# Seven products of halves in batch 1 as well, with the state read and the next scores moved behind stage 1's second tile

## The chip, the cores and the metric

The kernel runs on one core of one Trainium2 chip. The metric is the device time of one execution in microseconds. TensorE multiplies matrices, VectorE and ScalarE do elementwise work and empty TensorE's result banks, SyncE (SP) and ScalarE issue DMAs, and the 16 DMA engines move the data.

## The reference

For each of 8 batches there is an attention of 512 tokens and 32 states in 8 heads of 64, both ways, and then a bilinear layer over all rows (tokens and states, 4608 of them):

```
scores  = x @ state.T / 8          # softmax over the states
xread   = softmax(scores) @ state
scores2 = state @ x.T / 8          # softmax over the tokens
sread   = softmax(scores2) @ x
rows    = concat(xread, sread)     # (4608, 512)
out     = ((rows @ w1) * (rows @ w2)) @ w3 @ w_out
```

The weights come as float64; the result is float32.

## The kernel before

**Products.** A float32 operand is split into two parts of a 32-bit format that TensorE takes at a higher rate: `split` makes `hi` by a cast on ScalarE (L97) and `lo` by a subtraction on VectorE (L98). One product of two operands is then three matmuls (lo by hi, hi by hi, hi by lo).

**Before the batches.** The weights are loaded and turned into float32 in a pool `pro` that is closed later, w3 @ w_out is multiplied once (`w34`, L542 and L555) and kept split as `wo`.

**A batch.** The attention of a batch (`attention_steps`) is a generator in steps: the scores as matmuls (`per_head`, L147), then softmax steps on VectorE and ScalarE (L187 to L216), then `at_hi` and `at_lo` (L221, L97, L98), and last a transpose of the other softmax (L228), whose blocks sixteen DMAs on SP put in their places (`move_blocks`, L171). The read of the state (`read_state`, L243) multiplies these blocks by the batch's tokens `x_s`; its result goes through two VectorE operations and sixteen more DMAs on SP into `sread`. The token softmax never meets the state alone: `sw_steps` multiplies state by w1 and w2 (four units, L147), and stage 1 multiplies `at` by that.

Stage 1 (`stage1_sums`, L310) makes 8 feature tiles of 128 features by 512 tokens, 12 matmuls each for w1 and w2 together; ScalarE copies one half out of the bank, and VectorE multiplies it by the other. Three pairs of banks (`two_banks`) go round among stage 1, the scores and the `sw_steps` units. Stage 2 multiplies the features by `wo`.

Batches 0 and 1 do stage 2 plainly: four token tiles of 24 matmuls of 512 columns (`stage2`, L324). Batches 2 to 7 (`fast_batch`) do it in seven products of halves (`stage2_quarters`, `product`, L428), Winograd's form of Strassen's scheme, with 24 matmuls of 256 columns each. That needs sums and differences of the features' quarters (S1 to S4, on VectorE) and of the weights' quarters (`combine_weights`, four calls in all, L371 and L377).

**Order.** TensorE and SP execute in the order in which the program traces their instructions. VectorE and ScalarE are ordered by a planner that goes by program order, readiness and priority; `high_priority` lifts the emptying of a bank.

In batch 0's stage 2 the side work of batch 1 stands between the token tiles (`side_steps(1)`): scores earlier, then batch 0's read, units 0 and 1, then the rest of batch 1's softmax with its block moves, then units 2 and 3. After the last token tile come the loads of batch 1's tokens (`load_tokens(1)`, L159) and of batch 2's `st` and `x_d` (`load_x(2)`, L153, L155). In batch 1 the read, the scores of batch 2 and all units stand behind stage 2's first token tile. In batches 2 to 7 the read, the next scores and the next loads stand behind stage 1's fourth tile, softmax steps behind the fifth and seventh, units 0 and 1 behind stage 2's first product, followed by the last softmax step, and units 2 and 3 behind the second product.

After batch 7, `state_rows` passes all 256 state rows through the same layer (L661, L662, L324).

Of the kernel before, what the change touches and what calls it, by code (L numbers as in the profile page):

```python
# [35 lines left out]
WARM = 15  # L36
PLAIN = 2

@with_exitstack
def attn_bilinear_kernel(  # L40
# [53 lines left out]
    def split(hi, lo, src):  # L94

        return (
            nc.scalar.copy(out=hi, in_=src),  # L97
            nc.vector.tensor_tensor(out=lo, in0=src, in1=hi.bitcast(F32), op=ALU.subtract),  # L98
        )
# [242 lines left out]

    def side_steps(b):


        if b == B:
            return [[reads[b - 1]], [], [], []]
        scores, reads[b], a2 = attention_steps(b)
        w = sw_steps(b)
        softmax = scores()  # L350
        first = partial(islice, softmax, 3)
        if b == 1:
            def rest():

                with tc.issue_after(stored[0].ins):
                    yield from softmax

            return [[first], [reads[0], w[0], w[1]], [], [rest], [w[2], w[3]], []]

        product = partial(islice, softmax, 1)  # L360
        loads = [partial(load_tokens, b), partial(load_x, b + 1)]
        return [[w[0], w[1], product, reads[b - 1], *loads, w[2], w[3], lambda: softmax], [], [], []]

# [3 lines left out]
    def combine_weights(k):  # L367

        raw = [tmp_tile() for _ in range(2)]
        for i, whole in enumerate(raw):  # L370
            nc.vector.tensor_tensor(  # L371
                out=whole, in0=wo["hi"][:, i * QF + k].bitcast(F32), in1=wo["lo"][:, i * QF + k].bitcast(F32), op=ALU.add
            )
        b11, b12, b21, b22 = (whole[:, half * HO:(half + 1) * HO] for whole in raw for half in range(2))
        t = late.tile([P, QF, HO], F32, name="r22")
        for j, (x, y) in enumerate(((b12, b11), (b22, t[:, 0]), (b22, b12), (b21, t[:, 1]))):
            nc.vector.tensor_tensor(out=t[:, j], in0=x, in1=y, op=ALU.subtract)  # L377
# [10 lines left out]

    def hidden_quarters(ps, ft, q):
        a_sb = tmp_tile()  # L390
        p, kk = divmod(ft, 2)
        first, second = slice(0, HT), slice(HT, S)
        with tc.high_priority():
            nc.scalar.copy(out=a_sb, in_=ps[:, 0])  # L394
            if ft < QF:
                if kk == 0:
                    q["raw"].append(main.tile([P, 2, NF], F32, name="g_x", bufs=2))
                nc.vector.tensor_tensor(out=q["raw"][p][:, kk], in0=a_sb, in1=ps[:, 1], op=ALU.mult)  # L398
            else:
                if ft == QF:  # L400
                    q["r22"] = late.tile([P, QF, HT], F32, name="r22")
                nc.vector.tensor_tensor(out=a_sb[:, first], in0=a_sb[:, first], in1=ps[:, 1, first], op=ALU.mult)  # L402
                nc.vector.tensor_tensor(out=q["r22"][:, ft - QF], in0=a_sb[:, second], in1=ps[:, 1, second], op=ALU.mult)
# [4 lines left out]
        if ft >= QF:  # L408
            split(*(t[:, kk] for t in q["a12"][p - 2]), a_sb[:, first])
            if kk:  # L410
                i = p - 2
                raw, r22 = q["raw"][i], q["r22"][:, 2 * i:2 * i + 2]
                nc.vector.tensor_tensor(out=raw[:, :, second], in0=raw[:, :, second], in1=r22, op=ALU.add)
                nc.vector.tensor_tensor(out=raw[:, :, first], in0=raw[:, :, second], in1=raw[:, :, first], op=ALU.subtract)
        elif kk:
            raw = q["raw"][p]
# [3 lines left out]
            split(*q["s3"][p], s3)  # L420

    def product(ps, a, w, fresh):
# [10 lines left out]

    def stage2_quarters(b, q, units):
        half = lambda o: slice(o * HO, (o + 1) * HO)
# [5 lines left out]
        def stored_quarter(o, rows, cols):  # L441
            for tt in range(2):
                first = (2 * rows + tt) * P
                nc.scalar.dma_start(out=out[b, first:first + P, half(cols)], in_=o[:, half(tt)])
# [9 lines left out]
        for i in range(2):  # L454
            split(*a22[i], q["r22"][:, 2 * i:2 * i + 2])
# [5 lines left out]
        s = [raw[:, :, 0:HT] for raw in q["raw"]]  # L461
        for i in range(2):
            split(*s2[i], s[i])
        product(bank_e, a22, t_part(3), False)
        for i in range(2):
            hi, lo = (t.bitcast(F32) for t in q["a12"][i])
            nc.vector.tensor_tensor(out=s[i], in0=hi, in1=s[i], op=ALU.subtract)  # L467
            nc.vector.tensor_tensor(out=s[i], in0=lo, in1=s[i], op=ALU.add)
        s1 = quarter_pairs()
        for i in range(2):  # L470
            split(*s1[i], q["raw"][i][:, :, HT:S])
        bank_d = two_banks()[:, 0]
# [5 lines left out]
        for i in range(2):  # L478
            last_split[:] = split(*s4[i], s[i])
        bank_c = bank()  # L480
# [8 lines left out]

    def fast_batch(b):  # L490
        q = {"raw": []}
        softmax = iter(())
        for ft in range(FT):
            hidden_quarters(stage1_sums(b, ft), ft, q)
# [20 lines left out]
    def batch_stage2(b, gs):  # L515
        side = side_steps(b + 1)
        for tt in range(NT):
            stage2(gs, tt, [(out[b, tt * P:(tt + 1) * P], 0, P)])
            run(side[tt])
            if tt in (1, 2):  # L520
                combine_weights(tt + 1)


    with tc.tile_pool(name="pro", bufs=2) as pro:
# [90 lines left out]
        for quarter in range(QT):  # L615
# [5 lines left out]
            if quarter == 1:  # L621
                side = side_steps(1)
            elif quarter == 2:
                run(side.pop(0))
# [7 lines left out]
        early_stage2(QT - 1)  # L632
        for tt in range(NT):
            dests = [(out[0, tt * P:(tt + 1) * P], 0, P)]
            if tt in early:
                store(acc[tt], dests)
            else:
                stage2(gs, tt, dests)
            run(side[tt])
        load_tokens(1)  # L640
        load_x(2)
    late = ctx.enter_context(tc.tile_pool(name="late", bufs=1))
    t_parts = {part: late.tile([P, 4, QF, HO], F32R, name=f"t_{part}") for part in ("hi", "lo")}


    def state_rows():
# [5 lines left out]
        for ft in range(FT):  # L652
            quarter, c = divmod(ft * P, NQ)
            ps = two_banks()
            for i in range(2):
# [7 lines left out]
            gs.append([g[:, :n] for g in new_g(ft)])  # L663
# [4 lines left out]
            nc.vector.tensor_tensor(out=sums[:, 0], in0=sums[:, 0], in1=sums[:, 1], op=ALU.mult)  # L668
            split(*gs[-1], sums[:, 0])
# [4 lines left out]
    for b in range(1, PLAIN):  # L674
        gs = []
        for ft in range(FT):
            stage1(b, ft, gs)
            if ft % 4 == 3:
                combine_weights(ft // 4)
        batch_stage2(b, gs)  # L680
    for b in range(PLAIN, B):
        fast_batch(b)
    with tc.issue_after(last_split[0].ins), tc.issue_after(last_split[1].ins):
# [45 lines left out]
```

## Time and profile before

| | |
|---|---|
| median of three runs | 497.1 us (496.81 to 497.45) |
| the profiled execution, its own time | 496.68 us |
| its span, first to last instruction | 494.9 us |
| mean granted TensorE clock | 0.999 |
| TensorE busy | 486.4 us (98%) |
| VectorE busy | 375.3 us (76%) |
| ScalarE busy | 238.8 us (48%) |

All times in the views are microseconds from the span's start, and about 1.8 us of the execution lie outside the span. "PE" is TensorE's matmuls, "PEld" its weight loads, "DVE" VectorE, "ACT" ScalarE, "SPq" the DMAs that SP issues. In the chain of waits, each row is a piece of the chain that ended last, with its start and its length. A timeline row has start, length, engine, line, operation, the tile written and those read, shapes and a count; in brackets stands how long the engine was idle before and what ended that. A row of groups ends with busy time, the mean ns of one, and the idle time before.

### The profile page before, as it was taken

The numbers are of one execution on the slowest core, as the hardware profiler recorded it, in microseconds if no ns is written. First come the engines' busy times: TensorE is split into PE (matmuls) and PEld (weight loads), VectorE is DVE, ScalarE is ACT, GpSimd is POOL, SyncE is SP. The second block draws the span as 40 slices with busy tenths as digits, with TensorE's granted clock in tenths as the row PEclk, the third lists the DMA queues.
The fourth block names the chain that finished last, engine by engine and source line by source line (L and its number), as shares of the span: only waits on it lengthen the run. The fifth ranks groups of instructions, "written<-read, shape, count | busy, mean of one in ns | idle before, by whom it ended". The sixth has DMA issues, their size and how long they took to land.

```text
span 494.9 us, 8790 instructions
## 1 busy us (share of the span) xinstructions
PE 486.4 (98%) x3486; PEld 376.0 (76%) x3486; DVE 375.3 (76%) x584; ACT 238.8 (48%) x371; POOL 0.2 (0%) x4
## 2 busy tenths in 40 slices
PE   8999999999999999999999999999999999999996
PEld 5444467777876868897789778977897888899885
DVE  5669896772679889956995799479948994687770
ACT  4767784443544346613651365137513751453650
POOL 0000000000000000000000000000000000000000
PEclk9999999999999999999999999999999999999999
DMA  8996971013500721430233033303330222001101
GB/s 340 363 386 228 366 280 31 13 47 77 187 8 19 235 50 41 160 110 3 88 114 108 2 110 99 101 3 107 112 90 2 91 52 78 4 3 46 42 1 42
DMA packets 55785, 52.48 MB, mean 106 GB/s; under 512 B 42688, under 2 KB 49856, under 8 KB 51136
## 3 DMA queue, kind: packets, MB, share of 16 engines
q1 hardware_dynamic: 47488, 43.27, 26.6%
q10 hardware_dynamic: 8256, 8.65, 5.0%
q8 instruction: 27, 0.44, 0.4%
q14 instruction: 14, 0.11, 0.1%
HBM read 38.27 MB, written 8.91 MB: 95 GB/s over the span
## 4 chain that ended last, share of the span: by engine, by line
PE 83%; DVE 9%; DMA 3%; ACT 2%; issue 1%; SPq 1%; ACTq 0%; DVEq 0%
PE ps L310 29%; PE ps_o L428 20%; PE ps_o L324 8%; PE ps L147 6%; PE ps_o L555 6%; PE ps L661 3%; PE ps L428 3%; PE ps_o L542 3%; PE ps L542 3%; DMA e<-work 2%; PE ps L662 2%; DVE work L187 1%; DVE m L204 1%; DVE m L190 1%; SPq L171 1%
## 5 line engine op out<-in xcount | busy, mean ns | idle before, releaser
L310 PE MATMUL ps<-at_lo,sw_hi 128*128 128x512 f32 x256 | 101.2, 395 | 0.8 <-ACT g_hi L97 0.8
L310 PE MATMUL ps<-at_hi,sw_hi 128*128 128x512 f32 x256 | 99.7, 390 | 0.0
L310 PE MATMUL ps<-at_hi,sw_lo 128*128 128x512 f32 x256 | 99.6, 389 | 0.0
L394 ACT COPY tmp<-ps 128x512 f32<-128x512 f32 x48 | 28.1, 588 | 89.1 <-PE ps L310 54.4
L310 PEld LDWEIGHTS ps<-at_lo,sw_hi 128*128 128x128 f32 x256 | 48.1, 188 | 17.3 <-DVE g_x L398 3.4
L310 PEld LDWEIGHTS ps<-at_hi,sw_lo 128*128 128x128 f32 x256 | 48.1, 188 | 10.1
L310 PEld LDWEIGHTS ps<-at_hi,sw_hi 128*128 128x128 f32 x256 | 48.1, 188 | 9.6 <-issue 0.2
L97 ACT CAST g_hi<-g_x 128x512 fp32r<-128x512 f32 x48 | 29.2, 621 | 39.5 <-DVE g_x L467 20.4
L398 DVE TENSOR_TENSOR g_x<-tmp,ps 128x512 f32<-128x512 f32 x24 | 16.4, 687 | 36.2 <-ACT tmp L394 36.2
L97 ACT CAST g_hi<-tmp 128x256 fp32r<-128x256 f32 (+1 forms) x54 | 27.1, 503 | 32.4 <-DVE tmp L402 16.8
L98 DVE TENSOR_TENSOR sw_lo<-ps,sw_hi 128x1024 fp32r<-128x1024 f32 (+1 forms) x34 | 38.3, 1149 | 5.2 <-ACT sw_hi L97 5.2
L98 DVE TENSOR_TENSOR g_lo<-g_x,g_hi 128x512 fp32r<-128x512 f32 x48 | 31.6, 682 | 3.1 <-ACT g_hi L97 2.8
L98 DVE TENSOR_TENSOR g_lo<-tmp,g_hi 128x256 fp32r<-128x256 f32 (+1 forms) x54 | 28.8, 535 | 6.2 <-ACT g_hi L97 5.6
L97 ACT CAST sw_hi<-ps 128x1024 fp32r<-128x1024 f32 (+1 forms) x34 | 31.3, 967 | 4.2 <-PE ps L147 4.1
L147 PE MATMUL ps<-w_sb,st 64*32 64x512 f32 (+1 forms) x544 | 31.4, 570 | 0.0
L428 PE MATMUL ps_o<-wo_lo,g_hi 128*128 128x256 f32 x144 | 29.6, 287 | 0.5 <-DVE tmp L438 0.5
L428 PE MATMUL ps_o<-t_lo,g_hi 128*128 128x256 f32 x144 | 29.5, 287 | 0.0
L428 PE MATMUL ps_o<-t_hi,g_hi 128*128 128x256 f32 x144 | 29.0, 283 | 0.0
L428 PE MATMUL ps_o<-wo_hi,g_hi 128*128 128x256 f32 x144 | 29.0, 283 | 0.0
L428 PE MATMUL ps_o<-wo_hi,g_lo 128*128 128x256 f32 x144 | 29.0, 283 | 0.0
L428 PE MATMUL ps_o<-t_hi,g_lo 128*128 128x256 f32 x144 | 29.0, 283 | 0.0
L555 PE MATMUL ps_o<-w_sb,w 128*128 128x512 f32 x64 | 28.5, 599 | 0.0
(113 smaller groups left out, 912.6 us busy)
## 6 DMA issues: line engine op xcount, KB each, us to landing
raw<-in_w_k_dram SPq DMA_DIRECT2D x8, 1024.0 KB, 6.8
x_d<-in_x_d_dram SPq DMA_DIRECT2D x8, 1024.0 KB, 7.0
raw<-in_w_dram SPq DMA_DIRECT2D x8, 1024.0 KB, 6.4
x_s<-in_x_s_dram SPq DMA_DIRECT2D x8, 1024.0 KB, 5.3
out_dram<-tmp ACTq DMA_DIRECT2D x48, 128.0 KB, 2.0
raw<-in_w3t_dram SPq DMA_DIRECT2D x4, 1024.0 KB, 7.5
e<-work SPq DMA_DIRECT2D x96, 32.0 KB, 2.0
sread<-turned SPq DMA_DIRECT2D x128, 4.0 KB, 1.7
```

The costliest lines, as they stand in the source:

```text
L97: nc.scalar.copy(out=hi, in_=src),
L98: nc.vector.tensor_tensor(out=lo, in0=src, in1=hi.bitcast(F32), op=ALU.subtract),
L147: nc.tensor.matmul(ps[j * NS:(j + 1) * NS, q], sts[b][rows, j], moving(rows, j), start=True, stop=True)
L310: nc.tensor.matmul(ps[:, i], w[:, kt, c:c + P], a[:, kt], start=(k == 0), stop=(k == 3 * KT - 1))
L324: nc.tensor.matmul(ps[:, :DO], g, wo[w][:, ft, :], start=(ft == 0 and k == 0), stop=(ft == FT - 1 and k == 2))
L394: nc.scalar.copy(out=a_sb, in_=ps[:, 0])
L398: nc.vector.tensor_tensor(out=q["raw"][p][:, kk], in0=a_sb, in1=ps[:, 1], op=ALU.mult)
L428: nc.tensor.matmul(ps[:, tt * HO:(tt + 1) * HO], g[:, tt * P:(tt + 1) * P], w(part, k), start=(fresh and k == 0 and n == 0 and tt == 0), s ...
L542: nc.tensor.matmul(w34_ps[i][:, :DO], chunks[k][:, DO + i * P:DO + (i + 1) * P], w_out[k], start=(k == 0), stop=(k == FT - 1),)
L555: nc.tensor.matmul(w34_ps[i][:, :DO], w3s[i][:, k * P:(k + 1) * P], w_out[k], start=(k == 0), stop=(k == FT - 1))
L661: nc.tensor.matmul(ps[:, i], wh[:, ks], sr[:, kt], start=(kt == 0), stop=False)
L662: nc.tensor.matmul(ps[:, i, :n], wl[:, ks], sr[:, kt, 1], start=False, stop=(kt == NP - 1))
```

## The change

`PLAIN` goes from 2 to 1, so batch 1 takes the seven products, and the path for plain batches after batch 0 goes away. The function for the others is now `quarter_batch`:

- The read of the batch and the scores and loads of the next stand behind stage 1's second tile, and softmax steps behind the third and the fifth.
- The last softmax step, with the block moves, stands behind units 2 and 3.
- Feature tiles 4 to 7 are multiplied whole into a tile of their own, `late`'s `raw`, and their first halves are split two at a time. S4 is one subtraction per pair in stage 1, in place of two in stage 2 (L467, L468).
- The pool `late` opens ahead of batch 0's stage 2, where three of the four weight combinations now stand, one behind each of its first three token tiles. The fourth stands behind the second tile of batch 1.
- The loads `load_tokens(1)` and `load_x(2)` still follow batch 0's stage 2. The loads in later batches move with the read.

```
-PLAIN = 2
+PLAIN = 1
...
-        t = late.tile([P, QF, HO], F32, name="r22")
+        t = late.tile([P, QF, S], F32, name="raw")[:, :, :HO]
...
-    def hidden_quarters(ps, ft, q):
-        a_sb = tmp_tile()
+    def hidden_quarters(a, b, ft, q):
...
+        if ft == QF:
+            q["late"] = late.tile([P, QF, S], F32, name="raw")
+        elif ft < QF and kk == 0:
+            q["raw"].append(main.tile([P, 2, NF], F32, name="g_x", bufs=2))
+        whole = q["raw"][p][:, kk] if ft < QF else q["late"][:, ft - QF]
         with tc.high_priority():
...
-                nc.vector.tensor_tensor(out=a_sb[:, first], in0=a_sb[:, first], in1=ps[:, 1, first], op=ALU.mult)
-                nc.vector.tensor_tensor(out=q["r22"][:, ft - QF], in0=a_sb[:, second], in1=ps[:, 1, second], op=ALU.mult)
+            nc.vector.tensor_tensor(out=whole, in0=a, in1=b, op=ALU.mult)
...
+            split(*q["a12"][i], half[:, :, first])
+            nc.vector.tensor_tensor(out=raw[:, :, second], in0=raw[:, :, second], in1=half[:, :, second], op=ALU.add)
+            nc.vector.tensor_tensor(out=raw[:, :, first], in0=raw[:, :, second], in1=raw[:, :, first], op=ALU.subtract)
+            nc.vector.tensor_tensor(out=half[:, :, first], in0=half[:, :, first], in1=raw[:, :, first], op=ALU.subtract)
...
-        run(units[:3])
+        run(units)
...
-        run(units[3:])
+        run(more)
...
-        for i in range(2):
-            hi, lo = (t.bitcast(F32) for t in q["a12"][i])
-            nc.vector.tensor_tensor(out=s[i], in0=hi, in1=s[i], op=ALU.subtract)
-            nc.vector.tensor_tensor(out=s[i], in0=lo, in1=s[i], op=ALU.add)
...
-    def fast_batch(b):
+    def quarter_batch(b):
         q = {"raw": []}
+        w = sw_steps(b + 1) if b + 1 < B else [lambda: None] * 4
...
-            if ft == QF - 1:
+            if ft == 1:
                 reads[b]()
                 if b + 1 < B:
                     scores, reads[b + 1], _ = attention_steps(b + 1)
...
-            elif ft in (QF, QF + 2):
+            elif ft in (2, 4):
                 next(softmax, None)
-
-        units = sw_steps(b + 1) if b + 1 < B else []
-        stage2_quarters(b, q, units[:2] + [lambda: softmax] + units[2:])
+            if b == PLAIN and ft == 1:
+                combine_weights(QF - 1)
+        stage2_quarters(b, q, w[:2], [*w[2:], lambda: softmax])
...
-        load_tokens(1)
-        load_x(2)
     late = ctx.enter_context(tc.tile_pool(name="late", bufs=1))
     t_parts = {part: late.tile([P, 4, QF, HO], F32R, name=f"t_{part}") for part in ("hi", "lo")}
 
+    for tt in range(NT):
+        dests = [(out[0, tt * P:(tt + 1) * P], 0, P)]
+        if tt in early:
+            store(acc[tt], dests)
+        else:
+            stage2(gs, tt, dests)
+        run(side[tt])
+        if tt + 1 < QF:
+            combine_weights(tt)
+    load_tokens(1)
+    load_x(2)
```

The last block stood inside the pool `pro` before, without `combine_weights`. `state_rows` takes its feature tiles a little later in the program; `batch_stage2` and its weight combinations are gone.

More of the change, by code (lines that the diff above doesn't have):

```diff
@@ L341, in attn_bilinear_kernel, with side_steps, rest @@
     reads = {}
[L343 to L349, printed above, removed]
-        softmax = scores()
[L351 to L362, printed above, removed]
+    def side_steps():
+        scores, reads[1], _ = attention_steps(1)
+        w = sw_steps(1)
+        softmax = scores()
+        def rest():
+            with tc.issue_after(stored[0].ins):
+                yield from softmax
+        return [[partial(islice, softmax, 3)], [reads[0], w[0], w[1]], [], [rest], [w[2], w[3]], []]
     QF = FT // 2
@@ L387, in by_two @@
         return t.rearrange("p (k n) -> p k n", k=2)
-    def hidden_quarters(ps, ft, q):
-        a_sb = tmp_tile()
+    def hidden_quarters(a, b, ft, q):
         p, kk = divmod(ft, 2)
         first, second = slice(0, HT), slice(HT, S)
-        with tc.high_priority():
[L394 to L403, printed above, removed]
+        if ft == QF:
[3 more added lines that the diff above has]
+        whole = q["raw"][p][:, kk] if ft < QF else q["late"][:, ft - QF]
+        with tc.high_priority():
+            nc.vector.tensor_tensor(out=whole, in0=a, in1=b, op=ALU.mult)
         if ft == 0:
@@ L407, in hidden_quarters @@
             q["a12"] = quarter_pairs()
[L408 to L416, printed above, removed]
+        if not kk:
+            return
+        raw = q["raw"][p % 2]
+        if ft < QF:
             split(*q["a11"][p], raw[:, :, first])
@@ L420, in hidden_quarters @@
             split(*q["s3"][p], s3)
+        else:
+            i = p - 2
+            half = q["late"][:, 2 * i:2 * i + 2]
+            split(*q["a12"][i], half[:, :, first])
+            nc.vector.tensor_tensor(out=raw[:, :, second], in0=raw[:, :, second], in1=half[:, :, second], op=ALU.add)
+            nc.vector.tensor_tensor(out=raw[:, :, first], in0=raw[:, :, second], in1=raw[:, :, first], op=ALU.subtract)
+            nc.vector.tensor_tensor(out=half[:, :, first], in0=half[:, :, first], in1=raw[:, :, first], op=ALU.subtract)
     def product(ps, a, w, fresh):
@@ L432, in product, with stage2_quarters @@
                     )
-    def stage2_quarters(b, q, units):
+    def stage2_quarters(b, q, units, more):
+        first, second = slice(0, HT), slice(HT, S)
         half = lambda o: slice(o * HO, (o + 1) * HO)
@@ L442, in stored_quarter @@
             for tt in range(2):
-                first = (2 * rows + tt) * P
-                nc.scalar.dma_start(out=out[b, first:first + P, half(cols)], in_=o[:, half(tt)])
+                start = (2 * rows + tt) * P
+                nc.scalar.dma_start(out=out[b, start:start + P, half(cols)], in_=o[:, half(tt)])
         bank_a = bank()
@@ L454, in stage2_quarters @@
         for i in range(2):
-            split(*a22[i], q["r22"][:, 2 * i:2 * i + 2])
-        run(units[3:])
+            split(*a22[i], q["late"][:, 2 * i:2 * i + 2, second])
+        run(more)
         product(bank_a, q["a12"], b_part(1, 0), False)
@@ L460, in stage2_quarters @@
         s2 = quarter_pairs()
-        s = [raw[:, :, 0:HT] for raw in q["raw"]]
         for i in range(2):
-            split(*s2[i], s[i])
+            split(*s2[i], q["raw"][i][:, :, first])
         product(bank_e, a22, t_part(3), False)
-        for i in range(2):
-            hi, lo = (t.bitcast(F32) for t in q["a12"][i])
-            nc.vector.tensor_tensor(out=s[i], in0=hi, in1=s[i], op=ALU.subtract)
-            nc.vector.tensor_tensor(out=s[i], in0=lo, in1=s[i], op=ALU.add)
         s1 = quarter_pairs()
         for i in range(2):
-            split(*s1[i], q["raw"][i][:, :, HT:S])
+            split(*s1[i], q["raw"][i][:, :, second])
         bank_d = two_banks()[:, 0]
@@ L478, in stage2_quarters @@
         for i in range(2):
-            last_split[:] = split(*s4[i], s[i])
+            last_split[:] = split(*s4[i], q["late"][:, 2 * i:2 * i + 2, first])
         bank_c = bank()
@@ L488, in stage2_quarters @@
         stored_quarter(m1, 0, 1)
-    def fast_batch(b):
+    def quarter_batch(b):
         q = {"raw": []}
+        w = sw_steps(b + 1) if b + 1 < B else [lambda: None] * 4
         softmax = iter(())
         for ft in range(FT):
-            hidden_quarters(stage1_sums(b, ft), ft, q)
-            if ft == QF - 1:
+            ps = stage1_sums(b, ft)
+            a_sb = tmp_tile()
+            with tc.high_priority():
+                nc.scalar.copy(out=a_sb, in_=ps[:, 0])
+            hidden_quarters(a_sb, ps[:, 1], ft, q)
+            if ft == 1:
                 reads[b]()
@@ L513, in run @@
                 pass
[L515 to L521, printed above, removed]
     with tc.tile_pool(name="pro", bufs=2) as pro:
@@ L621, in attn_bilinear_kernel @@
             if quarter == 1:
-                side = side_steps(1)
+                side = side_steps()
             elif quarter == 2:
@@ L632, in attn_bilinear_kernel @@
         early_stage2(QT - 1)
[L633 to L639, printed above, removed]
-        load_tokens(1)
-        load_x(2)
     late = ctx.enter_context(tc.tile_pool(name="late", bufs=1))
     t_parts = {part: late.tile([P, 4, QF, HO], F32R, name=f"t_{part}") for part in ("hi", "lo")}
+    for tt in range(NT):
+        dests = [(out[0, tt * P:(tt + 1) * P], 0, P)]
+        if tt in early:
+            store(acc[tt], dests)
+        else:
+            stage2(gs, tt, dests)
[4 more added lines that the diff above has]
+    load_x(2)
     def state_rows():
@@ L668, in state_rows @@
             nc.vector.tensor_tensor(out=sums[:, 0], in0=sums[:, 0], in1=sums[:, 1], op=ALU.mult)
+            gs.append([g[:, :n] for g in new_g(ft)])
             split(*gs[-1], sums[:, 0])
@@ L671, in state_rows @@
             stage2(gs, tt, [(out[tt * PER + q, S:], q * NS, NS) for q in range(PER)])
[L674 to L680, printed above, removed]
     for b in range(PLAIN, B):
-        fast_batch(b)
+        quarter_batch(b)
     with tc.issue_after(last_split[0].ins), tc.issue_after(last_split[1].ins):
```

1 line of the change is left out of this document (removed).

## The prediction

> **What bounds the kernel now.** I read the page's first part first, then the chain of waits in order of time, then each engine's timeline around the places that the diff touches.
>
> ```profile
> span 494.9 us, 8790 instructions
> PE 486.4 (98%) x3486; PEld 376.0 (76%) x3486; DVE 375.3 (76%) x584; ACT 238.8 (48%) x371; POOL 0.2 (0%) x4
> ```
>
> TensorE works for 98% of the span, so time is won only by giving it less to do or by closing the few places where it waits; it executes in the order written, so one waiting matmul holds everything behind it. The chain, whose columns are start, length and what, shows what a batch costs:
>
> ```profile
> 119.47 21.76 PE ps L310 x96
> 141.23 5.44 PE ps_o L324 x24
> ...
> 178.84 1.90 DMA e<-work
> 180.88 1.05 PE ps_o L243 x58
> 181.94 1.02 PE ps L147 x16
> ...
> 194.06 2.87 PE ps_o L428 x24
> ...
> 198.81 3.07 PE ps_o L428 x24
> ...
> 203.75 5.95 PE ps_o L428 x48
> 209.71 2.88 PE ps L428 x24
> 212.59 5.76 PE ps_o L428 x48
> 218.35 10.92 PE ps L310 x48
> ...
> 267.15 10.92 PE ps L310 x48
> ```
>
> Batch 1, the plain one, starts stage 1 at 119.47; batch 3 starts at 218.35 and batch 4 at 267.15. A batch of seven products therefore takes 267.15 - 218.35 = 48.80 us, and batches 1 and 2 together 218.35 - 119.47 = 98.88. Batch 2 also waits for blocks of its attention (the DMA that ends at 180.74, ahead of the read at L243).
>
> **The change, part by part.** *Seven products in batch 1.* Four token tiles at 5.44 us make 21.76; the seven products above make 2.87 + 3.07 + 5.95 + 2.88 + 5.76 = 20.53. The gain is thus near 1.2 us, and the same comes out of whole batches: two regular ones take 2 x 48.80 = 97.60 against 98.88, a term of -1.28 us, with batch 2's wait in it. It is small: stage 1 and the softmax products do not shrink.
>
> *The read and the scores behind the second tile.* In batches 2 to 7 this moves the same matmuls 5.44 us earlier. In batch 1 it moves them out of stage 2, where the plain kernel has the read:
>
> ```profile
> 149.34 1.10 PE L243 MATMUL ps_o<-x_s,work 128*32 128x64 f32 x64
> ```
>
> The new place is after 24 stage-1 matmuls, at 119.47 + 5.44 = 124.91 us, 24 us earlier. What must be there? The read takes the token tile x_s of batch 1, the scores take x_d of batch 2. Both loads stand on SP's queue behind batch 0's stage 2, before and after the change, so their place in that queue is what counts (start, length; then KB each and us from issue to landing):
>
> ```profile
> 104.21 10.08 SPq L171 DMA_DIRECT2D sread<-turned  x16
> 114.87 10.67 SPq L171 DMA_DIRECT2D work<-work  x16
> 125.58 0.60 SPq L159 DMA_DIRECT2D x_s<-in_x_s_dram  x1
> ...
> 126.70 0.43 SPq L155 DMA_DIRECT2D x_d<-in_x_d_dram  x1
> ```
>
> ```profile
> x_s<-in_x_s_dram SPq DMA_DIRECT2D x1, 1024.0 KB, 5.5
> x_d<-in_x_d_dram SPq DMA_DIRECT2D x1, 1024.0 KB, 7.0
> ```
>
> SP issues back to back from 104.21: sixteen moves of batch 0's read result, sixteen block moves of batch 1's attention, then the loads. x_s lands at 125.58 + 5.5 = 131.1 and x_d at 126.70 + 7.0 = 133.7. The diff moves neither the loads nor the 32 moves ahead of them. So TensorE, there at 124.91, waits to 131.1 for the read, works 1.05, and waits from 132.2 to 133.7 for the scores. Without waits tile 2 would start at 124.91 + 1.05 + 1.02 = 126.98; with them at about 133.75 + 1.02 = 134.8. The term is **+7.8 us**, once. Queued behind the waiting read are the other 72 stage-1 matmuls of batch 1. This gap was covered before by six more tiles and a token tile of stage 2. Sixteen sread moves of batch 1 then follow the loads on SP, and after them the loads for batch 2, which have until batch 2's second tile.
>
> *The clock.* A wait of 6.2 us is long enough that the granted clock matters. The trace shows a fall after the last matmul and a slow start:
>
> ```profile
> 490.90:492.00 1.10, 0.00 (x0) 0.00 (x0) 0.00 (x0) 0.57 (x1) 0.00 (x0) 1.00 0.00 0
> 493.80:494.80 1.00, 0.00 (x0) 0.00 (x0) 0.00 (x0) 0.00 (x0) 0.00 (x0) 0.50 0.00 0
> ...
> 3.00:4.00 1.00, 1.00 (x7) 1.00 (x7) 1.00 1.00 426
> 5.60:6.60 1.00, 1.00 (x11) 1.00 (x9) 1.00 0.97 410
> ```
>
> In the first two rows (window, length, PE, PEld, DVE, ACT, POOL, clock, DMA share, GB/s) no matmul is under way from 490.9 on, and the clock is 1.00 there and 0.50 at 493.8: at most 2.9 us without a matmul halve it. In the last two, for the warm-up matmuls of L77 alone (PE, PEld, clock, DMA), about 7 go through per us at first and 11 in the microsecond after 5.60 (the clock column does not show this start): about 4.6 us of work came before the faster rate. A stop of 6.2 us should thus halve the clock, and work resumes at half rate for some 4.6 us. Counted from the read at 131.1 that reaches 135.7, and what is lost is half of the 2 us after 133.7, 1.0 us (the read is hidden by the second wait); counted from 133.7 half of 4.6, 2.3 us. I take **+1.7**; the bounds are 0 (the clock holds) and 3.4 (twice the price).
>
> The Trainium skill ("TensorE: Matmul & The Clock Gate", Part 1) says that the clock falls to half after an idle window of about 3.4 us and comes back after one busy window of that length, the windows running free. By its figures alone the estimate would be half of 3.4 to 6.8 us, so 1.7 to 3.4 us. The rows above agree with the halving, and show a fall a little earlier than a full window.
>
> *Weights combined in batch 0's stage 2.* Three of the four combinations go from batch 1 into batch 0's stage 2, one behind batch 1's second tile. Each is two additions, four subtractions, a cast on ScalarE and a subtraction:
>
> ```profile
> L371 DVE TENSOR_TENSOR tmp<-wo_hi,wo_lo 128x512 f32<-128x512 f32 x8 | 5.4, 680 | 0.0
> L377 DVE TENSOR_TENSOR r<-tmp,r 128x256 f32<-128x256 f32 x8 | 3.3, 415 | 0.0
> L98 DVE TENSOR_TENSOR t_lo<-r,t_hi 128x1024 fp32r<-128x1024 f32 x4 | 4.9, 1225 | 3.0 <-ACT t_hi L97 3.0
> ...
> 108.10 1.23 DVE L98 TENSOR_TENSOR at_lo<-work,at_hi 128x1024 fp32r<-128x1024 f32 x1 [1.67 <-ACT at_hi L97]
> 109.24 1.24 DVE L228 STREAM_TRANSPOSE work<-e 128x1024 f32<-128x1024 f32 x1
> ...
> 106.40:122.80 16.40, 16.40 (x97) 12.26 (x96) 4.75 (x5) 5.21 (x7) 0.00 (x0) 1.00 0.30 80
> ```
>
> That is 2 x 0.68 + 4 x 0.42 + 1.23 = 4.3 us, 12.8 for three, and VectorE idles 16.40 - 4.75 = 11.7 us in the window of the last row. The first one stands ahead of batch 1's last softmax steps and can hold the transpose at 109.24, which feeds the block moves. That transpose ends at 110.48, and SP comes free only at 114.87, so 4.4 us of delay cost nothing: term 0, bounds 0 and +4 (a second combination ahead of it, past that cover).
>
> *Less VectorE work per batch.* Tiles 4 to 7 lose two half-width multiplies for one whole, and S4 loses two operations of each pair for one:
>
> ```profile
> L402 DVE TENSOR_TENSOR tmp<-tmp,ps 128x256 f32<-128x256 f32 x24 | 9.9, 412 | 4.1 <-ACT tmp L394 4.0
> L398 DVE TENSOR_TENSOR g_x<-tmp,ps 128x512 f32<-128x512 f32 x24 | 16.4, 687 | 36.2 <-ACT tmp L394 36.2
> L467 DVE TENSOR_TENSOR g_x<-g_hi,g_x 128x512 f32<-128x512 f32 x12 | 8.2, 680 | 0.1
> ```
>
> 4 x (0.41 + 0.41 - 0.69) + 2 x 0.68 = 1.9 us per batch, off the critical engine. It can only act where TensorE waits on VectorE, and a regular batch has one such place:
>
> ```profile
> 236.58 0.39 PE L310 MATMUL ps<-at_hi,sw_lo 128*128 128x512 f32 x1
> 237.17 0.47 PE L310 MATMUL ps<-at_lo,sw_hi 128*128 128x512 f32 x1 [0.20 <-ACT g_hi L97]
> 236.61 0.41 DVE L403 TENSOR_TENSOR r<-tmp,ps 128x256 f32<-128x256 f32 x1
> ```
>
> The second tile after the scores starts 0.59 after the matmul before it instead of 0.23, because the multiplies of the tile two ahead end at 237.02, behind the scores' transpose and reductions. After the change the scores again follow an odd tile, whose pair is split by the same operations, so I expect the same queue and the same 0.4 us: term 0. It can go (-0.4 in up to six batches, -2.4) or double (+2.4). In batch 1 the long wait lets VectorE get ahead and it falls away: -0.4.
>
> **Sum.** -1.28 + 7.8 + 1.7 - 0.4 = +7.8 us. The span of 494.9 becomes 502.7, the profiled execution's 496.68 becomes 504.5; the median of the runs, 497.1, lies 0.4 above that execution, so I predict **504.9 us**.
>
> **Rivals.** *Faster: the loads are there in time.* If x_s and x_d were landed by 125 us, because SP gets to them 6 to 9 us earlier, only -1.28 stays and perhaps the 0.4 of each regular batch: 497.1 - 1.3 = 495.8, down to 493.4. It decides once the loads are issued before about 118 us. Against it: the two trains of moves take 10.08 + 10.67 us of SP time whatever VectorE does, and stand ahead of the loads in the code. 0.10. (With another 0.02 for a result within 0.2%, which is about what can be told from no change here.)
>
> *The clock holds.* Then only the wait counts: 504.9 - 1.7 = 503.2. For it: the 1.1 us stop of batch 2 left no mark; against it the end of the trace. 0.20.
>
> *The block moves come later still.* If the combinations hold the transpose beyond 114.87, the loads shift with it, one for one: up to +4, 509. Against it stand the 4.4 us. 0.08.
>
> *A wait in every batch.* The read is now due 5.44 us into stage 1, while the softmax's last step stands two units later in stage 2:
>
> ```profile
> 300.99 1.23 DVE L228 STREAM_TRANSPOSE work<-e 128x1024 f32<-128x1024 f32 x1
> 302.28 11.77 SPq L171 DMA_DIRECT2D e<-work  x16
> 315.94 10.92 PE ps L310 x48
> ```
>
> The sixteen moves end near 314.1 + 1.9 = 316.0 with the landing time quoted above, and the new read would be due at 315.94 + 5.44 = 321.4: 5.4 us of cover. The two units in front take 1.88 us of TensorE and two splits of some 1.2 us on VectorE, so I expect a delay of 2 to 4. If it is 7.4, each of six batches waits 2 us: 504.9 + 12 = 517. 0.06.
>
> **How the numbers follow.** My forecast has 0.54, the clock that holds 0.20, and both lie in one interval with the uncertain 0.4 us per batch: from 503.2 - 1.7 = 501.5 to 504.9 + 1.7 + 1.7 = 508.3. That leaves out the faster case, the wait in every batch and the end of the late moves, about 0.2 together. Faster 0.11, same 0.02, slower 0.87.
>
> **What would show it.** In the profile after: a gap of TensorE near 125 us that ends with the landing of x_s, a second one that ends with x_d, both loads still issued near 125.6, a clock share under 1.0 in the slices just after, batch 1's products in L428's rows, and about 48.8 us from batch to batch from batch 2 on, without the wait at 178.8. Wrong would be loads issued well ahead of 118 us, a read that starts at 125 us, or waits at L243 in the later batches.

## The result, and the profile after

The changed kernel takes 504.64 us (median of 5 runs, 504.20 to 505.97) against 496.96 of the kernel before (5 runs, 496.69 to 497.45): 1.0157 of its time, 95% interval 1.0141 to 1.0172. It is slower by 7.7 us; the forecast was 504.9. The profiled span is 502.9 against 494.9.

The page of the changed kernel, its totals and two rows of slices:

```profile
span 502.9 us, 8937 instructions
PE 488.3 (97%) x3558; PEld 379.5 (75%) x3558; DVE 376.8 (75%) x555; ACT 239.1 (48%) x364; POOL 0.2 (0%) x4
...
PE   8999999999489999999999999999999999999996
...
PEclk9999999999799999999999999999999999999999
```

TensorE's busy time hardly moved, 486.4 to 488.3, while the span grew by 8. One slice of 40 (126 to 138 us) carries it: TensorE at 4 tenths, the clock at 7. The chain of waits around that place (start, length, what), where SP's block moves L171 lead into it:

```profile
125.87 0.61 SPq L171
...
126.58 5.54 DMA x_s<-in_x_s_dram
132.13 0.25 issue
132.38 2.49 PE ps_o L243 x64
...
138.56 1.22 DVE t_lo L98
139.78 1.16 DVE work L187
140.94 1.11 DVE m L190
142.05 1.12 DVE m L204
143.17 0.60 DVE g_x L391
143.78 0.04 issue
143.82 11.17 PE ps L310 x48
...
179.28 5.47 PE ps L310 x24
...
227.91 5.47 PE ps L310 x24
```

A train of moves, then the load of x_s, then the read: that is the chain which the prediction drew. A second piece, VectorE from 138.6 to 143.8, was not in it. Batch 2 then takes 227.91 - 179.28 = 48.63 us. SP's timeline shows the queue:

```profile
104.74 10.08 SPq L171 DMA_DIRECT2D sread<-turned  x16
114.94 11.54 SPq L171 DMA_DIRECT2D e<-work  x16
126.58 0.54 SPq L159 DMA_DIRECT2D x_s<-in_x_s_dram  x1
...
127.64 0.43 SPq L155 DMA_DIRECT2D x_d<-in_x_d_dram  x1
```

The 32 moves and the loads stand in the same order as before, the loads 1.0 us later, and stage 1 of batch 1 begins 0.5 us later (119.84 against 119.31). One thing about the moves is new: the tile that takes the blocks goes by `PLAIN` too (L229), so batch 1's sixteen block moves write `e`, as in the later batches, where they wrote `work` before; they take 11.54 us here instead of 10.67 (why was not tried). TensorE's timeline (in brackets the idle time before, and what ended it), and below it the windows of the same stretch (length, PE, PEld, DVE, ACT, POOL, clock, DMA share, GB/s):

```profile
125.06 0.39 PE L310 MATMUL ps<-at_hi,sw_lo 128*128 128x512 f32 x1
132.38 2.48 PE L243 MATMUL ps_o<-x_s,e 128*32 128x64 f32 x64 [6.93 <-DMA x_s<-in_x_s_dram]
134.93 1.66 PE L147 MATMUL ps<-x_d,st 64*32 64x512 f32 x16
136.52 0.50 PE L310 MATMUL ps<-at_lo,sw_hi 128*128 128x512 f32 x1
```

```profile
125.40:129.30 3.90, 0.05 (x1) 0.00 (x0) 3.16 (x5) 1.82 (x3) 0.00 (x0) 1.00 0.43 85
129.30:136.10 6.80, 3.64 (x80) 2.42 (x80) 1.23 (x5) 0.00 (x0) 0.00 (x0) 0.50 0.70 287
136.20:139.00 2.80, 2.80 (x19) 2.06 (x12) 1.65 (x5) 1.05 (x1) 0.00 (x0) 1.00 0.04 7
```

TensorE waits 6.93 us, and read and scores run at half clock (129.33 to 136.16 in the trace's clock records).

Feature tiles are counted from 0 here, so the read stands between tiles 1 and 2. The table lists the length of each batch, from its first stage-1 matmul to the next batch's (batch 7: to the first matmul of the state rows), as the traces have it. It serves all experiments below.

| kernel | batch 0 | 1 | 2 | 3 to 6, each | 7 | span |
|---|---|---|---|---|---|---|
| before | 52.5 | 49.44 | 49.43 | 48.80 | 43.96 | 494.9 |
| before, second trace | 54.0 | 49.44 | 49.68 | 48.80 to 48.97 | 43.19 | 496.1 |
| after | 53.1 | 59.28 | 48.63 | 48.63 | 43.19 | 502.9 |
| filler ahead of the read | 52.6 | 56.75 | 48.67 | 48.63 | 43.19 | 500.1 |
| fourth combination earlier | 52.6 | 58.07 | 48.66 | 48.65 | 43.20 | 501.4 |
| read behind the fourth tile | 53.8 | 51.32 | 48.70 | 48.70 | 43.19 | 496.0 |
| loads ahead of the block moves | 53.5 | 57.55 | 48.65 | 48.65 | 43.19 | 501.9 |
| loads first | 53.1 | 49.13 | 48.65 | 48.64 | 43.20 | 493.4 |
| sixth tile in batch 1 | 52.9 | 49.26 | 48.67 | 48.65 | 43.19 | 492.7 |
| loads first, fourth combination earlier | 53.1 | 50.11 | 48.67 | 48.64 | 43.20 | 493.8 |
| place of the read alone | 53.3 | 49.44 | 57.31 | 48.65 | 43.20 | 502.1 |
| S4 by two operations | 52.6 | 59.61 | 48.63 | 48.63 | 43.20 | 502.7 |

From before to after, batch 1 grows by 9.84 us, and all else together shrinks by 1.9 (batch 0 +0.5, batch 2 -0.80, batches 3 to 6 -0.68, batch 7 -0.77, the rest -0.15).

### The profile page after: what moved, and what is told of

The parts are those of the page before. It is cut to its first block, busy times and chain, and to the rows that moved or that the text cites. A ratio compares the mean times of both kernels' runs of the same rounds, so it can differ in the third digit from the quotient of the medians.

```text
span 502.9 us, 8937 instructions
## 1 busy us (share of the span) xinstructions
PE 488.3 (97%) x3558; PEld 379.5 (75%) x3558; DVE 376.8 (75%) x555; ACT 239.1 (48%) x364; POOL 0.2 (0%) x4
## 4 chain that ended last, share of the span: by engine, by line
PE 78%; DVE 8%; SPq 6%; ACT 4%; DMA 2%; issue 1%; DVEq 0%; ACTq 0%
PE ps L310 29%; PE ps_o L418 24%; SPq L171 6%; PE ps L147 5%; PE ps L418 4%; PE ps L646 3%; PE ps_o L525 3%; PE ps L525 3%; PE ps_o L324 3%; PE ps_o L243 2%; PE ps L647 2%; DVE w_sb L134 1%; DMA x_s<-in_x_s_dram 1%; ACT ulps L126 1%; DMA raw<-in_w_k_dram 1%
## 5 line engine op out<-in xcount | busy, mean ns | idle before, releaser
L310 PEld LDWEIGHTS ps<-at_hi,sw_lo 128*128 128x128 f32 x256 | 48.1, 188 | 10.2
L418 PE MATMUL ps_o<-t_lo,g_hi 128*128 128x256 f32 x168 | 34.5, 287 | 0.0
L418 PE MATMUL ps_o<-wo_lo,g_hi 128*128 128x256 f32 x168 | 34.4, 286 | 0.0
L98 DVE TENSOR_TENSOR g_lo<-raw,g_hi 128x512 fp32r<-128x512 f32 x42 | 28.6, 687 | 7.0 <-ACT g_hi L97 6.3
L418 PE MATMUL ps_o<-wo_hi,g_hi 128*128 128x256 f32 x168 | 33.8, 283 | 0.0
L418 PE MATMUL ps_o<-t_hi,g_hi 128*128 128x256 f32 x168 | 33.8, 283 | 0.0
L418 PE MATMUL ps_o<-wo_hi,g_lo 128*128 128x256 f32 x168 | 33.8, 283 | 0.0
L418 PE MATMUL ps_o<-t_hi,g_lo 128*128 128x256 f32 x168 | 33.8, 283 | 0.0
L97 ACT CAST g_hi<-raw 128x512 fp32r<-128x512 f32 x42 | 25.0, 619 | 17.8 <-DVE raw L391 7.2
L418 PEld LDWEIGHTS ps_o<-wo_lo,g_hi 128*128 128x128 f32 x168 | 26.6, 191 | 5.6 <-ACT tmp L443 5.0
L418 PEld LDWEIGHTS ps_o<-t_lo,g_hi 128*128 128x128 f32 x168 | 26.1, 192 | 5.0 <-issue 5.0
```

The source lines that it names most:

```text
L310: nc.tensor.matmul(ps[:, i], w[:, kt, c:c + P], a[:, kt], start=(k == 0), stop=(k == 3 * KT - 1))
L418: nc.tensor.matmul(ps[:, tt * HO:(tt + 1) * HO], g[:, tt * P:(tt + 1) * P], w(part, k), start=(fresh and k == 0 and n == 0 and tt == 0), s ...
```

## The experiments

Where no number of runs is given, an experiment is one profiled execution, and is read batch by batch from the table above.

**TensorE kept busy ahead of the read.** In batch 1:

```
             if ft == 1:
+                if b == PLAIN:
+                    filler = bank()
+                    hi = at_tiles[b][0]
+                    for _ in range(27):
+                        nc.tensor.matmul(filler, hi[:, 0, :P], hi[:, 1], start=True, stop=True)
                 reads[b]()
```

> 27 matmuls of 128x512 whose result nobody uses stand ahead of batch 1's read, some 6.1 us of TensorE work in place of its idle wait. Theory (the wait is for x_s, and the halved clock makes the read 2.5 us and the scores 1.6 us): the clock stays at 1.0, the read takes 1.05 from about 132.4, then the wait for x_d that the slow read hid comes out, scores from about 134.6 in 1.02, tile 2 at about 135.6 instead of 136.5; span 502.0 instead of 502.9. Rival (the read is long because of its data or of its banks, not of the clock): read 2.5 and scores 1.6 as before, span 502.9.

Span 500.1, 1.9 under the forecast. TensorE's timeline, and two rows of VectorE's:

```profile
131.97 1.65 PE L243 MATMUL ps_o<-x_s,e 128*32 128x64 f32 x64 [0.71 <-DMA x_s<-in_x_s_dram]
134.53 1.09 PE L147 MATMUL ps<-x_d,st 64*32 64x512 f32 x16 [0.91 <-DMA x_d<-in_x_d_dram]
135.55 0.50 PE L310 MATMUL ps<-at_lo,sw_hi 128*128 128x512 f32 x1
...
132.20 1.23 DVE L98 TENSOR_TENSOR t_lo<-raw,t_hi 128x1024 fp32r<-128x1024 f32 x1 [1.11 <-ACT t_hi L97]
133.66 0.29 DVE L248 TENSOR_TENSOR scaled<-ps_o,sum 128x128 f32<-128x128 f32 x1 [0.24 <-PE ps_o L243]
```

The clock holds, and the wait for x_d, which the slow read had filled, comes out. Stage 1's start to tile 2 takes 135.55 - 119.54 = 16.0 us instead of 136.52 - 119.84 = 16.7: the clock's own price at this place is 0.7 us. The read takes 1.65, not the 1.05 expected; that part of its length is not the clock. The batch became 2.5 us shorter, though, not 0.7. VectorE's order explains the rest: in this trace the planner placed the whole fourth combination ahead of the operation that waits for the read, and it ran during the wait. With that a gap of 1.95 us at tile 4 is gone, down to 0.23, which the next experiment is about.

**The fourth combination earlier.**

```
-        if tt + 1 < QF:
-            combine_weights(tt)
+        combine_weights(tt)
...
-            if b == PLAIN and ft == 1:
-                combine_weights(QF - 1)
```

> The fourth combination of weights stands behind batch 0's fourth token tile instead of behind batch 1's second tile. Theory (its 4.3 us on VectorE hold back the scores' transpose and reductions, and with them the multiply that frees the banks for tile 4): the gap of 1.95 us at batch 1's tile 4 falls to the 0.37 of the later batches, span 501.3. Rival (the scores themselves, late after the wait, hold the banks): the gap stays above 1.5, span 502.9.

Span 501.4, near the theory's 501.3. In the changed kernel 1.95 us lie between the start of tile 3's last matmul and that of tile 4's first; here it is 0.23, an ordinary step. The gap and its cause, in TensorE's and VectorE's timelines of the changed kernel:

```profile
141.87 0.39 PE L310 MATMUL ps<-at_hi,sw_lo 128*128 128x512 f32 x1
143.82 0.50 PE L310 MATMUL ps<-at_lo,sw_hi 128*128 128x512 f32 x1 [1.56 <-DVE g_x L391]
...
128.63 0.69 DVE L98 TENSOR_TENSOR g_lo<-tmp,g_hi 128x512 fp32r<-128x512 f32 x1
134.89 0.29 DVE L248 TENSOR_TENSOR scaled<-ps_o,sum 128x128 f32<-128x128 f32 x1 [5.57 <-PE ps_o L243]
...
138.56 1.22 DVE L98 TENSOR_TENSOR t_lo<-raw,t_hi 128x1024 fp32r<-128x1024 f32 x1 [1.12 <-ACT t_hi L97]
139.70 1.24 DVE L187 STREAM_TRANSPOSE work<-ps 128x1024 f32<-128x1024 f32 x1
```

VectorE sat idle for 5.57 us behind the read's result, with most of the combination queued after it, and did that work when the scores were waiting. The gain is partly returned: the clock stayed at one half for 10.2 us here (127.35 to 137.59) instead of 6.8, into tile 2, which takes 3.5 us instead of 2.85. So batch 1 is 1.2 us shorter, not 1.7, and that the span still meets the forecast is due to batch 0, which is 0.4 shorter.

**The read behind the fourth tile in all batches**, softmax steps behind the fifth and seventh:

```
-            if ft == 1:
+            if ft == 3:
...
-            elif ft in (2, 4):
+            elif ft in (4, 6):
```

> Read, scores and loads behind the fourth tile in all batches, softmax steps behind the fifth and seventh, the rest as changed. Theory (TensorE waits for the landing of x_s near 132.1 and of x_d near 134.5): in batch 1 it arrives at 130.8, waits 1.6 for x_s, reads in 1.03 at full clock, waits 1.1 for x_d; the loss at that place falls from 9.1 to about 2.8 us, and the combination no longer stands ahead of the scores, another 1.6: span 495.0 from these two, with 0.17 more in each of six batches if the place of the read is what made batches 48.63 instead of 48.80, so 495 to 496. Rival (seven products in batch 1 cost more than the plain form for a reason of their own): batch 1 stays above 56 us and the span above 500.

Span 496.0, batch 1 51.32: the rival falls. Two short waits remain, and the clock holds:

```profile
132.91 1.65 PE L243 MATMUL ps_o<-x_s,e 128*32 128x64 f32 x64 [1.37 <-DMA x_s<-in_x_s_dram]
135.49 1.09 PE L147 MATMUL ps<-x_d,st 64*32 64x512 f32 x16 [0.92 <-DMA x_d<-in_x_d_dram]
```

**The loads ahead of the block moves on SP**, the read still behind the second tile:

```
-        return [[partial(islice, softmax, 3)], [reads[0], w[0], w[1]], [], [rest], [w[2], w[3]], []]
+        loads = [partial(load_tokens, 1), partial(load_x, 2)]
+        return [[partial(islice, softmax, 3)], [reads[0], *loads, w[0], w[1]], [], [rest], [w[2], w[3]], []]
...
-    load_tokens(1)
-    load_x(2)
```

> The loads of x_s and x_d stand between the read's sixteen moves and the sixteen block moves on SP, the read stays behind the second tile. Theory (the whole queue counts, both trains and the loads): x_s lands near 121 and x_d near 123, but the block moves now start near 116.8 and the last lands near 129.8, so the read waits from 125.4 to about 129.9 for that, in full for its last part; no wait at the scores; the clock may hold. Loss at this place 4 to 5.5 us instead of 9.1, span 498 to 499.5. Rival (the loads alone are the cause): the read starts at 125.4, span 493.8.

Span 501.9: the rival is wrong, since the read now waits for the blocks, but the theory's 4 to 5.5 us are wrong as well; the loss stays near 8.7 (136.83 - 120.54 = 16.3 to tile 2, against 7.6 in a batch without waits). SP, then TensorE:

```profile
118.35 13.35 SPq L171 DMA_DIRECT2D e<-work  x16
...
126.86 0.27 PE L243 MATMUL ps_o<-x_s,e 128*32 128x64 f32 x2 [0.71 <-DMA e<-work]
127.91 0.27 PE L243 MATMUL ps_o<-x_s,e 128*32 128x64 f32 x2 [0.78 <-DMA e<-work]
130.59 0.27 PE L243 MATMUL ps_o<-x_s,e 128*32 128x64 f32 x2 [2.41 <-DMA e<-work]
133.12 1.89 PE L243 MATMUL ps_o<-x_s,e 128*32 128x64 f32 x58 [2.26 <-DMA e<-work]
```

The moves start 3.4 us later than in the changed kernel (0.7 of it because batch 1 starts later) and take 13.35 instead of 11.54 us. Most issues still take about 0.6 us. But the first block, moved while x_s and x_d were loading, took 7.5 us to land instead of the median of 2.0, and SP stood still for its landing before the eighth move, as the chain of waits has it:

```profile
118.35 7.49 DMA e<-work
```

The theory had no such delay. The read goes piece by piece as blocks land, and these few matmuls did not keep the clock up (one half from 131.17 to 138.00).

**Loads first.** The loads as in the last experiment, and in addition the sixteen moves of batch 0's read result go behind the block moves. Their source tile gets a second buffer, and the tile before it goes from two to one (not shown):

```
-            turned = att.tile([P, KT, D], F32, name="turned", bufs=1)
+            turned = att.tile([P, KT, D], F32, name="turned", bufs=2)
...
+        late_moves = lambda: first_a2["moved"]()
+        return [[partial(islice, softmax, 3)], [reads[0], *loads, w[0], w[1]], [], [rest], [late_moves, w[2], w[3]], []]
```

> SP's queue reordered: the loads of x_s and x_d right behind batch 0's read, then batch 1's sixteen block moves, and the sixteen moves of batch 0's read result behind them (the tile they read from has two buffers, the one before it one). The read stays behind the second tile. Theory (only the place in SP's queue holds the read): x_s lands near 110, the last block near 125, so the read starts at 125.4 to 125.8 and the scores follow at full clock; 9.1 us fewer, less up to 2.5 that the fourth combination can cost once VectorE has no wait to catch up in: 495.6 to 498. Rival (the read behind the second tile is too early for VectorE or the blocks whatever the queue does): a wait of over 3 us at the read remains, over 499.

494.54 us (5 runs): 0.9955 of the kernel before, interval 0.9942 to 0.9967, a little under the range of the theory. SP, and the read that starts as soon as tile 1 is done:

```profile
102.88 0.34 SPq L159 DMA_DIRECT2D x_s<-in_x_s_dram  x1
...
104.59 0.43 SPq L155 DMA_DIRECT2D x_d<-in_x_d_dram  x1
112.47 11.52 SPq L171 DMA_DIRECT2D e<-work  x16
124.04 21.01 SPq L171 DMA_DIRECT2D sread<-turned  x32
...
125.99 1.10 PE L243 MATMUL ps_o<-x_s,e 128*32 128x64 f32 x64
```

Not one matmul or byte is fewer than in the changed kernel, and 10 us are gone: the order on SP was the cause.

**Batch 1's read behind its sixth tile**, the queue as changed:

```
-            if ft == 1:
+            if ft == (5 if b == PLAIN else 1):
...
-            elif ft in (2, 4):
+            elif ft in ((6, 7) if b == PLAIN else (2, 4)):
```

> Batch 1 alone has its read, scores and loads behind the sixth tile (softmax steps behind the seventh and eighth); later batches as changed. Theory: TensorE arrives at about 136.4, after x_s and x_d have landed, no wait and no clock loss, and the fourth combination is done long before: 504.6 - 9.1 - 1.6 = 494. Batch 2's blocks come some 4 us later than with the second tile, which its read still hides or pays with up to 1 us. Rival (the late softmax of batch 2 turns into a wait of its own at batch 2's stage 1 or read): 496 to 498.

494.70 us (5 runs), 0.9956 of before, interval 0.9943 to 0.9968. So the change pays, by 0.4%, in two ways, by an earlier load or by a later read. Which of the two is better can't be told.

**Loads first and the fourth combination earlier**, the two edits above together.

> The reordered queue and the fourth combination behind batch 0's fourth token tile, together. Theory (two causes that add): every batch from 1 on takes 48.6 us, 504.6 - 9.1 - 1.6 = 494, 3 us under the kernel before. Rival (VectorE, with four combinations in batch 0's stage 2, holds the transpose that feeds the block moves, or the first multiplies of batch 1): 495.5 or more.

495.55 us (8 runs), 0.9977 of before, interval 0.9963 to 0.9990. The rival is right, by the time and by its second mechanism: the causes don't add. Without a wait in which VectorE can catch up, four combinations in batch 0's stage 2 put it behind in batch 1's first tiles, and TensorE pays at tile 4 again (a gap of 1.73 us; the row of waits, and VectorE's multiply of tile 1, 9.0 us after stage 1's start instead of 6.3 in loads first):

```profile
PE ps L315 <- DVE g_x L398: 1.3, 1, 1.3
```

```profile
127.75 1.23 DVE L98 TENSOR_TENSOR t_lo<-raw,t_hi 128x1024 fp32r<-128x1024 f32 x1 [1.11 <-ACT t_hi L97]
128.89 0.68 DVE L398 TENSOR_TENSOR g_x<-tmp,ps 128x512 f32<-128x512 f32 x1
```

**The place of the read alone**, in the kernel before (batch 1 plain):

```
-            if ft == QF - 1:
+            if ft == 1:
...
-            elif ft in (QF, QF + 2):
+            elif ft in (2, 4):
...
-        stage2_quarters(b, q, units[:2] + [lambda: softmax] + units[2:])
+        stage2_quarters(b, q, units[:2] + units[2:] + [lambda: softmax])
```

(`run(units[:3])` and `run(units[3:])` become `units[:2]` and `units[2:]`.)

> The kernel before with one part of the change: in batches 2 to 7 the read, scores and loads stand behind the second tile, softmax steps behind the third and fifth, the last step behind units 2 and 3; batch 1 stays plain. Theory (the place of the read turns any late arrival into a wait, wherever it is): batch 2's blocks land near 180.8 in the kernel before, and TensorE is there 5.4 us earlier, at about 174.3, so its wait grows from 1.1 to 6.5 us and the clock may halve (up to 2 us more): batch 2 takes 54.8 to 57 us instead of 49.4. Batches 3 to 6 go from 48.80 to about 48.73 (the 0.07 that the place is worth), span about 500 to 502. Rival (only batch 1's loads were the trouble): batch 2 takes at most 49.4, span at most 494.9.

Span 502.1, batch 2 57.31 us, just over the range. The wait moved to the first batch that has its read early, as the theory has it: batch 1 is plain here and keeps its 49.44, so seven products in batch 1 aren't needed for the loss. What comes late is different, though, batch 2's blocks and not a load. Waits of TensorE and SP's queue:

```profile
PE ps_o L243 <- DMA e<-work: 5.5, 3, 2.1
```

```profile
167.55 12.41 SPq L171 DMA_DIRECT2D e<-work  x16
```

Batches 3 to 6 take 48.65, so the place alone is worth 0.15 us per batch; the 0.07 expected was too low.

**S4 by two operations again**, the two loops of the diff put back in stage 2, the one subtraction taken out.

> The changed kernel with S4 again by two operations per pair in stage 2, in place of one in stage 1. Theory (one subtraction instead of two closes the 0.77 us wait of batch 7's last product and part of the 0.17 per regular batch): batch 7 to the state rows takes 43.96 again, regular batches 48.65 to 48.75, span 503.7 to 504.4. Rival (the whole multiplies and the splits two at a time did it): 43.19 and 48.63 as in the changed kernel, span 502.9.

48.63 and 43.20, the rival's numbers: S4 makes no difference to batches 2 to 7. That the whole multiplies made them shorter isn't shown by this; the place of the read (above) and the next trace account for most of it. (Batch 1 came out at 59.61, as the clock was at one half for 10.2 us here.)

**The kernel before, traced again.** No edit.

> The kernel before, unchanged, for a second trace. Theory (the length of batch 0, 52.5 in the trace of before and 52.6 to 53.8 in the traces of changed kernels, scatters with SP's block moves near 84 us and is no effect of the change): another value in that range, with every batch from 1 on as in the first trace, 49.44, 49.43 and 48.80. Rival (the change lengthens batch 0): 52.5 again.

Batch 0 takes 54.0, a little above the expected range, and batch 7 43.19. Both differences between the traces of before and after, +0.5 in batch 0 and -0.77 in batch 7, thus lie within what two executions of one kernel differ by. Batches 2 to 6 differ by up to 0.25 as well, but batches 3 to 6 are never under 48.80 in the two traces of the kernel before, and always under it with the change. SP's last block moves of batch 0, which VectorE waits for at the scores, ended at 90.15 here, and at 88.62 in the first trace:

```profile
79.63 10.52 SPq L171 DMA_DIRECT2D work<-work  x15
91.55 1.25 DVE L187 STREAM_TRANSPOSE work<-ps 128x1024 f32<-128x1024 f32 x1 [2.68 <-DMA work<-work]
```

In the first trace that transpose started at 90.00, 1.55 us earlier.

## Why the prediction was right

- **The wait for the loads, +7.8.** Shown. At full clock (filler ahead of the read) tile 2 starts 16.0 us after stage 1's start, against 186.73 - 179.12 = 7.6 in batch 2: 8.4 us. Of the 0.6 more than predicted nearly all is SP's: from its first `sread` move to the load of x_s it took 21.9 us in that run (126.38 - 104.44) instead of 21.4 (125.58 - 104.21). The prediction took 10.67 us for the block moves from the old kernel, where they write `work`, though they write `e` after the change. Loads first and the read behind the sixth tile each take the wait away, and the place alone brings such a wait to another batch.
- **The clock, +1.7.** The halving is shown, the size was too large: 0.7 at that place. The term that was too large is the 4.6 us of work until the clock is back, counted, for the higher of its two estimates, from the scores. The slow stretch lasted 6.83 us in all; 3.05 of it passed in the wait for x_s, the read's part lay under the wait for x_d, and the clock was back 3.8 us after the read began, 0.4 before the scores were done. The lower of the two estimates, 1.0, was near. Where the stretch lasts 10.2 us it reaches tile 2 and costs more.
- **VectorE gets ahead in the wait, -0.4.** This step failed. The gap at tile 4 grew to 1.95 us instead of the 0.37 of later batches, +1.6: VectorE did not work ahead, as it stood behind the read's result with the fourth combination queued behind. The prediction put no price on the fourth combination, and had not looked at what is ahead of it in VectorE's order. Where the planner put it ahead (filler ahead of the read), the gap did fall to 0.23.
- **Seven products and a regular batch 1, -1.28.** With the waits taken away (loads first; sixth tile) batch 1 is 49.13 to 49.26 instead of 49.44, with one wait for VectorE of 0.3 to 0.6 us still in it, and batch 2 is 48.65 to 48.67 instead of 49.43. That makes 1.0 to 1.1 us, part of it from the place of the read, too little to carry any wait, as predicted.
- **Batches as before, 0 each.** They became 0.17 shorter (48.80 to 48.63). The place of the read alone gives 0.15 (48.65). With the read back behind the fourth tile and all else as changed they take 48.70, as the gap at tile 6 falls from 0.59 to 0.44 us; so the rest of the change is worth 0.10 there. The two don't add, and which part of the rest it is was not tried.
- **Combinations in batch 0's stage 2, 0.** Right: SP's block moves start at 114.94 against 114.87. A fourth one there doesn't delay them either (114.56), but without a wait behind it VectorE carries it into batch 1's first tiles.
- The errors of +2.0 us at tile 4 and +0.6 at the load were offset by the clock (-1.0), the later batches with what follows them (-1.0) and the scatter of batches 0 and 7 (-0.25). That the total came within 0.3 us is luck; that the wait is most of it is not.

Of the rivals, the wait in every batch and the later block moves did not come, and the clock did not hold. The faster case became real only in the kernels that move the loads or the read.

## What to carry to other kernels

Before a consumer is moved up on an in-order engine, look up when each of its inputs lands, and walk the DMA queue back from there: here 32 small moves, 21.8 us on SP (104.74 to 126.58), stood ahead of two loads that nobody had needed so early. Reordering a queue so that what is due first is issued first was worth more, 10 us, than the saved arithmetic, about 1 us. Work counted on to fill a wait fills it only if it does not stand, on its own engine, behind something that waits for the same thing.

## What the runs showed of the hardware

- **The slow clock comes in steps.** In the clock records, the half-rate stretches last 6.83 us (after; loads ahead of the block moves; place alone) or 10.24 us (fourth combination earlier; S4 by two operations), two or three times 3.41. The stretches at full clock between them are whole multiples as well (122.88 is 36 times, 365.23 is 107 times). This agrees with the Trainium skill ("TensorE: Matmul & The Clock Gate", Part 1: free-running windows of about 3.4 us).
- **Where the work falls in such a step decides.** Cut into steps of 3.41 us, the traces show the clock fall at the end of one with no work in it (after, 125.92 to 129.33) and also of one with 1.1 us of work (fourth combination earlier, 123.94 to 127.35), so 3.9 and 2.3 us after the last matmul; one with 2.1 us kept it up (place alone, from 173.40). At half clock a step with 2.5 us of work didn't bring it back (fourth combination earlier, from 130.76), and one with 3.3 did (after, from 132.75). Single waits of 1.4 us (read behind the fourth tile) and 1.6 us (after, at tile 4) left the clock alone.
- **Small moves beside large loads land late.** With 2 MB of loads in flight, one block of 32 KB took 7.5 us to land (median 2.0), SP waited for it, and sixteen moves took 13.35 us to issue. In the other changed kernels, with these loads landed or not yet issued, they took 11.5 to 11.9. Batch 2's moves, issued right behind two loads in the place alone and in both traces of before, took 12.4 to 12.8.
- **The read is slower right behind its load.** At full clock it took 1.65 us in two kernels where it starts as x_s lands and x_d is still loading, and 1.10 where both had landed long before. Why was not tried.
